# A gated mix of a long convolution and an MLP: the same operations in another order on every engine, with other PSUM banks

## The chip, the cores and the metric

The kernel runs on one core of a Trainium2 chip. The metric is the device time of one execution in microseconds (us). The kernel's five queues are those of TensorE (PE, matmuls and transposes), ScalarE (ACT, activations and copies), VectorE (DVE, elementwise work), GpSimd (POOL) and SyncE (SP, which only issues transfers). ACT and POOL issue transfers too. Each queue is worked off in its order, and an instruction whose semaphore isn't there yet holds up all that stand behind it in its queue.

## The reference

From a sequence of S = 2048 rows of D = 640 channels the kernel computes two results `a` and `b`, and mixes them with a gate `g` of each row. `a` is a short causal filter along the sequence (4 taps), times `v`, then a long convolution along the sequence by FFT, times `q`. `b` is a mixer: layer norm, a matrix, GELU, a shift by one or two rows of each quarter of the channels, a matrix, and then an MLP of width 1536.

```python
def _A_ref(q, k, v, shift_k, ssm_k, ssm_D):
    ...
    for t in range(ks):
        k_shift = k_shift + k_pad[:, t:t + S, :] * shift_k[:, ks - 1 - t][None, None, :]
    kv = k_shift * v
    ...
    y_f = kv_f * kf_f[None, :, :, :]
    y = (lambda x, s, axes=(-2,-1): jnp.fft.irfft2(x, s=s, axes=axes).astype(jnp.bfloat16))(y_f, (1, L), axes=(1, 2))[:, 0, :S, :]
    y = y + kv * ssm_D[None, None, :]
    return q * y

def _B_ref(x, w1, w2, w3, w4):
    h = _gelu(_layernorm(x, axis=-1) @ w1)
    ...
    hs = jnp.concatenate([g0, g1, g2, g3], axis=-1) @ w2
    x1 = x + hs
    h2 = _gelu(_layernorm(x1, axis=-1) @ w3) @ w4
    return x1 + h2

x = A_q
g = _sigmoid((x * gate_w).sum(-1, keepdims=True))
a = _A_ref(x, A_k, A_v, A_shift_k, A_ssm_k, A_ssm_D)
b = _B_ref(x, B_w1, B_w2, B_w3, B_w4)
return g * a + (1 - g) * b
```

## The kernel before

The kernel is recorded first and ordered afterwards. Calls such as `ln1`, `mm1`, `h_fold` or `final` record operations, numbered from 0 to 1199 in the order of the calls; each has its engine, its function and its predecessors (who wrote what it reads, who still reads what it overwrites). An operation of PE can hold several matmuls. The helpers `mm` (L635), `act` (L625), `tt` (L615), `ts` (L620) and `dma` (L238) record nearly all of it, so that the profile shows these few lines; an operation is told from another by its shape, and below by its number.

The stages, by the names of the calls:

- `x_load`, `ln1`, `mm1`, `mmg`, `gate`: rows of `q` are loaded, normalised (statistics on DVE, the power on POOL), turned by PE transposes whose copies ACT makes (`pe_turn`, L846), multiplied by w1 (4 chunks of 512 rows) and put through GELU by ACT. PE first runs 28 warm-up matmuls (L658), and a tiny sum of the gate's weights (`gsum`).
- `h_load`, `h_fold`, `h_chunk` (5 blocks of 128 channels): the transform of the long filter as matmuls with folded cosine and sine tables; `kv_load`, `kv_fold`, `x_fwd` the same for the filtered `k` times `v`: taps on ACT, sums and folds on DVE, a transposing transfer on SP, matmuls on PE, copies on ACT. `combine` folds blocks in the frequency domain on DVE.
- `mm2`, `ln2` (16 tiles of 128 rows): the second matrix, the residual on DVE, the second layer norm on ACT, DVE and POOL, and a transposing transfer on SP.
- `mm3` (4 chunks of 512 rows, 12 tiles of 5 matmuls of 512 columns, GELU on ACT) and `mm4` (16 tiles of 128 rows, two halves of 12 or 13 matmuls of 320 columns). A chunk's mm4 needs its mm3, and the next chunk's mm3 overwrites what mm4 reads. ACT scales the result by 1 − g, and POOL adds it to the output with an accumulating transfer; `base` puts the residual there before.
- `unit(hh, c)`: the products of the spectra on DVE for one half hh of the channels, the sums by accumulating transfers of POOL.
- `final(hh, c, q, k)`: 16 blocks, 8 for each half hh. In one block PE makes two inverse halves of four matmuls each (a PSUM tile of two banks, class `inv`), ACT copies them to SBUF, DVE forms the sum and the difference, PE reverses the rows of the difference with one matmul (the flip, a PSUM tile of one bank, class `fl`), ACT copies that with the gate's scale, and DVE multiplies by `q`. For k < 12 POOL adds the block to the output, for k ≥ 12 DVE adds the residual and SP stores the block.

Of the last blocks these numbers matter below. final(0, 1, 0): 1078 copy of the inverse, 1079 sum, 1080 difference, 1081 flip, 1082 the flip's copy, 1083 the multiplication. 1092 and 1093 are flip and copy of final(0, 1, 1), with 1094 its multiplication; 1116 is the multiplication of final(0, 0, 1). From 1118 on all belong to hh = 1: 1136 and 1137 are the inverse halves of final(1, 2, 0) and 1138 their copy; 1127 and 1128 those of final(1, 3, 1). 1020, 1021, 1026 and 1027 are DVE's last operations of the spectral products for hh = 1. 960 and 961 are the halves of the last mm4 tile, 962 its copy.

What the order comes from: `SEQUENCE` (L452 to L515) lists all 1200 numbers by hand; each engine's queue is this list, cut to that engine. `PLACES` (L517 to L522) gives each of the 213 PSUM tiles, in the order of recording, its first bank of eight. `schedule` (L255) walks the list and makes the first matmul of a tile wait for all users on other engines of the tile that had its banks before:

```python
for b in range(t.place, t.place + t.n):
    if tenant[b] is not None:
        for u in tenant[b].users:
            if ops[u].eng != "pe":
                o.preds.setdefault(u, False)
    tenant[b] = t
```

`emit` (L276) writes the queues with a semaphore wait for each predecessor on another engine that isn't known to be done already. So both lists set waits: the one by what stands ahead in the same queue, the other by the banks.

Of the kernel before, what the change touches and what calls it, by code (L numbers as in the profile page):

```python
# [414 lines left out]
def bass_gated_mix__ssm_conv_h3__mixer_s_mlp__prompt_kernel(  # L415
# [32 lines left out]
    def ps(n, cls):  # L448
# [3 lines left out]
    SEQUENCE = [40, 58, 3, 1, 38, 8, 41, 59, 7, 6, 5, 9, 42, 4, 2, 0, 39, 60, 10, 11, 61, 12, 46, 13, 43, 141, 14, 15, 142, 16,  # L452
# [672 lines left out]

    sched = P.schedule(SEQUENCE, PLACES)
    with nc.Block() as block:  # L1127
# [29 lines left out]
```

## Time and profile before

| | us |
|---|---|
| three runs | 231.78, 232.71, 232.36 |
| median | 232.36 |
| the profiled execution | 232.63 |
| its span in the trace | 230.84 |
| busy in it: PE, DVE, ACT, POOL | 216.46, 210.77, 185.74, 73.06 |
| waiting times of ACT for PE (L635), of PE's weight loads for ACT | 24.7, 13.6 |

The profile's page gives busy times and, in its fourth part, the chain of work that ended last, followed back from the last instruction. A timeline has one row for each run of like instructions: start, length, engine, line, operation, output and input, count, and in brackets the idle time before it with what ended that. A table of windows has for each stretch of time the busy time of the engines with the number of instructions in brackets, then the granted clock of PE (1.00 is full), the share of the transfer engines and GB/s. Groups of instructions have the count, then the busy time with the mean in ns of one, then the idle time just before them. PEld is the weight load that overlaps the matmuls. Matmuls are pipelined, so that one's recorded length is more than the step from its start to the next one's.

### The profile page before, as it was taken

What the parts mean: (1) busy time and instruction counts of PE and PEld (TensorE: products, weight loads), DVE (VectorE), ACT (ScalarE), POOL (GpSimd) and SP (SyncE); (2) the same over time, 40 slices, a digit from 0 to 9 for tenths busy, and PEclk for the clock granted to TensorE, in tenths of its full rate; (3) what the DMA queues carried; (4) which work ended last, traced back from release to release, by engine and by line L of the source; (5) the groups of instructions that cost most, each with busy time, mean ns of one, the idle gap of its engine ahead of it and who ended that gap; (6) DMA issues with size and microseconds to landing.
All of it is one profiled execution on the core that took longest, in us unless ns stands there. A gap on an engine that the chain in (4) does not pass through costs nothing.

```text
span 230.8 us, 3937 instructions
## 1 busy us (share of the span) xinstructions
PE 216.5 (94%) x1455; PEld 127.2 (55%) x1455; DVE 210.8 (91%) x372; ACT 185.7 (80%) x352; POOL 73.1 (32%) x76
## 2 busy tenths in 40 slices
PE   6998899999999999999999999999999999999960
PEld 2576564674464454444765457654666645677630
DVE  5997699999899988979889999999998999999892
ACT  2289869999999999999979878967998368354990
POOL 1223000070230210320295205173118135255962
PEclk9999999999999999999999999999999999999995
DMA  5999948987596999985399776899949949999997
GB/s 180 389 240 265 228 173 151 284 199 165 99 218 180 156 198 275 304 186 122 75 203 189 201 142 126 134 181 208 298 101 183 214 97 164 187 165 118 110 145 141
DMA packets 73937, 42.67 MB, mean 185 GB/s; under 512 B 53945, under 2 KB 69182, under 8 KB 73918
## 3 DMA queue, kind: packets, MB, share of 16 engines
q1 hardware_dynamic: 64912, 30.55, 53.7%
q0 software_dynamic: 8832, 11.80, 34.0%
q8 instruction: 11, 0.18, 0.3%
q10 hardware_dynamic: 174, 0.07, 0.2%
q14 instruction: 8, 0.07, 0.1%
HBM read 14.88 MB, written 6.55 MB: 93 GB/s over the span
## 4 chain that ended last, share of the span: by engine, by line
PE 69%; ACT 26%; DVE 2%; issue 1%; DVEq 0%; ACTq 0%
PE PSall L635 65%; ACT arena L625 26%; PE PSall L658 3%; DVE arena L615 1%; PE PSall L846 1%; DVE arena L655 0%; DVEq L1127 0%; PE PSall L690 0%; DVE arena L646 0%; DVE arena L648 0%; ACTq L364 0%; DVE arena L662 0%
## 5 line engine op out<-in xcount | busy, mean ns | idle before, releaser
L635 PE MATMUL PSall<-arena 128*128 128x320 bf16 (+4 forms) x1341 | 204.2, 310 | 4.6 <-ACT arena L625 2.2
L635 PEld LDWEIGHTS PSall<-arena 128*128 128x128 bf16 x1341 | 119.8, 98 | 87.4 <-ACT arena L625 13.6
L615 DVE TENSOR_TENSOR arena<-arena 128x2560 bf16<-128x2560 bf16 (+7 forms) x201 | 162.8, 861 | 4.9 <-ACT arena L625 2.0
L625 ACT ACTIVATE arena<-PSall 128x512 bf16<-128x512 f32 (+9 forms) x187 | 107.5, 636 | 19.4 <-PE PSall L635 11.1
L625 ACT ACTIVATE arena<-arena 128x1 f32<-128x1 f32 (+5 forms) x115 | 69.5, 646 | 4.0 <-DVE arena L615 2.2
L816 POOL TENSOR_TENSOR arena<-arena 128x1 f32<-128x1 f32 (+1 forms) x26 | 24.1, 954 | 71.5 <-DVE arena L620 71.4
L238 POOL DMA_DIRECT2D out_dram<-arena x28 | 31.3, 1241 | 37.9 <-ACT arena L625 32.9
L625 ACT ACTIVATE arena<-PSall,arena 128x640 bf16<-128x640 f32 (+1 forms) x32 | 20.3, 658 | 13.7 <-PE PSall L635 13.6
L620 DVE TENSOR_SCALAR arena<-arena 128x640 bf16<-128x640 bf16 (+6 forms) x75 | 24.8, 361 | 3.9 <-ACT arena L625 2.8
L238 POOL DMA_DIRECT2D arena<-arena x12 | 16.6, 1384 | 29.9 <-DVE arena L615 29.9
L914 DVE SCALAR_TENSOR_TENSOR arena<-PSall,arena 128x640 bf16<-128x640 f32 x16 | 13.0, 819 | 3.8 <-PE PSall L635 3.8
L812 DVE BATCH_NORM_STATS2 arena<-arena 128x6 f32<-128x320 bf16 x32 | 14.4, 481 | 1.5 <-DMA arena<-in_A_q_dram 1.5
L658 PE MATMUL PSall<-arena 128*128 128x512 bf16 x28 | 9.7, 478 | 1.8 <-DVE arena L655 1.8
L846 PE MATMUL PSall<-arena 128*128 128x128 bf16 x80 | 7.1, 220 | 1.5 <-ACT arena L625 1.3
L846 PEld LDWEIGHTS PSall<-arena 128*128 128x128 bf16 x80 | 5.1, 97 | 3.7 <-ACT arena L625 2.7
L620 POOL TENSOR_SCALAR arena<-arena 128x16 f32<-128x16 f32 x3 | 2.6, 856 | 11.3 <-ACT arena L625 11.3
L658 PEld LDWEIGHTS PSall<-arena 128*128 128x128 bf16 x28 | 2.9, 116 | 5.0 <-issue 2.5
L615 POOL TENSOR_TENSOR arena<-arena 128x16 f32<-128x16 f32 x3 | 4.2, 1391 | 2.4 <-DVE arena L620 2.2
L625 ACT ACTIVATION_READ_ACCUMULATOR arena<-arena 128x1 f32 x16 | 3.5, 218 | 0.0
L664 ACT ACT_TABLE_LOAD x1 | 1.3, 1283 | 2.1 <-issue 2.1
L813 DVE BATCH_NORM_AGGREGATE arena<-arena 128x2 f32<-128x12 f32 x16 | 2.6, 192 | 0.2
L914 DVE DVE_READ_ACCUMULATOR arena<-PSall,arena 128x1 f32 x16 | 1.3, 82 | 0.0
(19 smaller groups left out, 3.4 us busy)
## 6 DMA issues: line engine op xcount, KB each, us to landing
arena<-arena POOLq DMA_DIRECT2D x12, 640.0 KB, 6.3
arena<-in_A_q_dram SPq DMA_DIRECT2D x14, 320.0 KB, 6.2
out_dram<-arena POOLq DMA_DIRECT2D x20, 160.0 KB, 4.4
arena<-in_A_ssm_k_dram SPq DMA_DIRECT2D x5, 512.0 KB, 5.2
arena<-in_B_w_dram SPq DMA_DIRECT2D x1, 1920.0 KB, 8.2
out_dram<-arena SPq DMA_DIRECT2D x10, 160.0 KB, 3.0
arena<-in_B_w_dram SPq DMA_DIRECT2D x1, 1152.0 KB, 6.2
out_dram<-arena SPq DMA_DIRECT2D x12, 80.0 KB, 2.8
```

The lines of the kernel that those rows point to most:

```text
L238: fn = lambda e: e.dma_start(out, in_, **kw)
L615: P.op(eng, lambda e: e.tensor_tensor(o, real(a), real(b), op), [a, b], [o], dve_ns(o, [a, b], 2) if eng == "dve" else 500)
L620: P.op(eng, lambda e: e.tensor_scalar(o, real(a), s1, s2, op0=op0, **({} if op1 is None else {"op1": op1})), [a] + aps, [o], dve_ns(o, [a] ...
L625: P.op("act", lambda e: e.activation(real(o), real(a), f, bias=bias, scale=scale, **({"accum_out": accum} if accum is not None else {})), ...
L635: fns.append(lambda e, l=l, r=r, i=i: e.matmul(real(o), l, r, start=(i == 0), stop=(i == last)))
L658: P.op("pe", lambda e: e.matmul(real(pw), warm[:, 0:128], warm[:, 128:640], start=True, stop=True), [warm], [pw], 427.0)
L664: P.op("act", lambda e: e.activation(tjunk[:, 1:2], ones[:, 0:1], ACTF.Gelu_apprx_tanh), [ones[:, 0:1]], [tjunk[:, 1:2]], 1700)
L812: P.op("dve", lambda e, o=o, i=i: e.bn_stats(o, i), [i], [o], 400)
L813: P.op("dve", lambda e: e.bn_aggr(bna[:, t, :], bns[k]), [bns[k]], [bna[:, t, :]], 120)
L816: P.op("pool", lambda g: g.tensor_tensor(o, a, e, ALU.pow), [a, e], [o], dur)
L846: P.op("pe", [lambda e, c=c, pb=pb, xn=xn: e.transpose(real(pb)[:, 128 * c:128 * (c + 1)], xn[:, 128 * c:128 * (c + 1)], ident) for c in r ...
L914: P.op("dve", lambda e: e.scalar_tensor_tensor(x, real(pr), 1.0, x, op0=ALU.mult, op1=ALU.add, accum_out=st[1, 0][:, t:t + 1]), [pr, x], [ ...
```

## The change

Both lists are replaced by others; no other line differs. `SEQUENCE` is another permutation of the same 1200 numbers that keeps every operation behind those it depends on. The median operation moves by 10 places and the farthest by 400. On PE 289 of 340 places of the queue hold another operation than before, on ACT 310 of 339, on DVE 308 of 356, on POOL 43 of 72, on SP 61 of 93. `PLACES` gives 174 of the 213 tiles another bank. Instructions, shapes, data and buffers in SBUF are the same.

The beginnings and the ends of the lists, the lines with ln2-11's and ln2-12's transfers (719 and 730) and the statistics of ln2-12 (726) among them, and the banks:

```diff
-    SEQUENCE = [40, 58, 3, 1, 38, 8, 41, 59, 7, 6, 5, 9, 42, 4, 2, 0, 39, 60, 10, 11, 61, 12, 46, 13, 43, 141, 14, 15, 142, 16,
-                17, 62, 18, 202, 19, 63, 327, 64, 68, 65, 305, 53, 69, 20, 66, 54, 21, 55, 203, 22, 67, 23, 70,
-                24, 49, 72, 56, 71, 78, 73, 51, 79, 25, 74, 26, 50, 27, 80, 28, 84, 75, 29, 52, 85, 94, 81, 96,
-                525, 82, 98, 100, 83, 143, 30, 76, 147, 31, 77, 146, 144, 102, 157, 104, 103, 145, 148, 105, 86,
-                106, 88, 57, 101, 87, 108, 47, 89, 160, 109, 32, 107, 33, 99, 91, 97, 110, 90, 149, 158, 150, 92,
-                161, 95, 34, 93, 35, 205, 136, 36, 306, 208, 113, 131, 111, 154, 114, 151, 119, 112, 155, 204,
...
-                813, 864, 723, 715, 716, 654, 726, 824, 865, 727, 717, 718, 804, 736, 655, 656, 805, 806, 708,
-                883, 657, 815, 928, 719, 877, 807, 670, 728, 757, 729, 929, 823, 730, 870, 878, 822, 866, 1030,
...
-                979, 1078, 1011, 1106, 1039, 1021, 960, 980, 1024, 981, 961, 1020, 1051, 1091, 1022, 1026, 1013,
-                1136, 962, 1079, 1114, 1127, 1080, 1115, 1128, 963, 1028, 1116, 1023, 1092, 1027, 1081, 1145,
-                1093, 1117, 1129, 1137, 1094, 1082, 1146, 1130, 1095, 1029, 1131, 1187, 1083, 1138, 1174, 1147,
-                1139, 1084, 1132, 1188, 1140, 1133, 1148, 1164, 1149, 1040, 1189, 1134, 1150, 1165, 1151, 1190,
-                1135, 1175, 1191, 1166, 1194, 1152, 1118, 1176, 1167, 1141, 1192, 1153, 1168, 1119, 1142, 1177,
-                1154, 1181, 1120, 1178, 1195, 1155, 1182, 1193, 1196, 1143, 1179, 1169, 1156, 1197, 1183, 1121,
-                1144, 1180, 1122, 1157, 1170, 1123, 1158, 1124, 1184, 1159, 1198, 1125, 1160, 1199, 1185, 1161,
-                1186, 1126, 1171, 1162, 1172, 1163, 1173]
-    PLACES = [0, 1, 1, 2, 6, 5, 3, 2, 3, 4, 5, 6, 7, 6, 7, 1, 4, 1, 0, 7, 5, 1, 6, 6, 3, 2, 0, 5, 5, 2, 4, 5, 0, 7, 6, 0, 6, 6,
-                2, 6, 6, 5, 7, 6, 3, 6, 3, 7, 2, 3, 7, 1, 0, 1, 0, 7, 1, 1, 1, 0, 4, 4, 6, 6, 0, 2, 2, 2, 6, 4, 4,
-                6, 4, 6, 4, 6, 2, 4, 2, 0, 2, 0, 0, 4, 0, 4, 4, 2, 0, 3, 5, 3, 2, 6, 2, 4, 4, 7, 3, 4, 6, 2, 2, 2,
-                4, 6, 4, 2, 0, 6, 0, 0, 6, 2, 6, 0, 0, 2, 2, 6, 0, 4, 0, 2, 6, 0, 0, 6, 6, 0, 0, 6, 6, 4, 2, 3, 4,
-                1, 4, 2, 5, 5, 5, 4, 0, 0, 2, 4, 6, 4, 5, 2, 5, 4, 3, 4, 5, 3, 2, 2, 4, 4, 2, 6, 6, 6, 2, 1, 3, 0,
-                7, 1, 7, 0, 1, 7, 6, 0, 2, 4, 2, 4, 7, 6, 2, 6, 0, 6, 4, 0, 6, 4, 7, 4, 6, 2, 7, 2, 3, 4, 2, 2, 0,
-                0, 2, 4, 2, 0, 2, 4, 0, 6, 1]
+    SEQUENCE = [40, 58, 8, 41, 3, 5, 0, 9, 59, 38, 2, 37, 1, 39, 10, 60, 11, 61, 12, 13, 42, 46, 43, 14, 141, 15, 16, 142, 17, 18,
+                62, 19, 203, 20, 63, 202, 64, 68, 65, 305, 53, 69, 21, 66, 55, 22, 54, 327, 23, 4, 24, 67, 7, 70,
+                51, 72, 71, 78, 73, 525, 79, 25, 74, 26, 27, 80, 28, 84, 75, 94, 85, 81, 96, 29, 82, 98, 100, 83,
+                147, 99, 76, 30, 146, 77, 31, 32, 86, 88, 56, 87, 101, 47, 57, 97, 143, 95, 110, 144, 89, 111,
+                145, 102, 161, 113, 33, 148, 34, 90, 91, 104, 149, 208, 92, 112, 150, 35, 207, 93, 36, 106, 209,
+                158, 108, 114, 131, 103, 151, 154, 152, 133, 308, 123, 153, 115, 48, 205, 127, 105, 160, 135, 155,
...
+                663, 686, 814, 864, 813, 723, 806, 726, 816, 734, 727, 865, 746, 712, 824, 882, 728, 729, 715,
+                866, 805, 730, 716, 871, 807, 815, 717, 718, 883, 958, 817, 719, 928, 822, 1041, 876, 884, 1030,
...
+                1009, 1037, 1077, 1038, 972, 968, 1091, 1008, 969, 973, 1024, 978, 1010, 974, 1011, 1078, 975,
+                1104, 1025, 979, 1105, 960, 1079, 980, 1027, 1106, 1026, 1029, 981, 1013, 961, 1039, 1012, 1051,
+                1021, 1080, 1023, 1020, 1092, 1081, 962, 1136, 1137, 1093, 963, 1028, 1127, 1094, 1138, 1128,
+                1095, 1082, 1187, 1129, 1083, 1188, 1139, 1022, 1140, 1145, 1084, 1189, 1130, 1141, 1131, 1146,
+                1142, 1190, 1174, 1194, 1147, 1195, 1040, 1132, 1191, 1175, 1196, 1143, 1133, 1164, 1148, 1176,
+                1134, 1144, 1165, 1149, 1177, 1118, 1135, 1178, 1166, 1181, 1150, 1119, 1182, 1151, 1167, 1183,
+                1154, 1168, 1120, 1152, 1169, 1155, 1170, 1121, 1153, 1179, 1122, 1192, 1156, 1171, 1123, 1124,
+                1172, 1180, 1173, 1125, 1193, 1157, 1184, 1126, 1158, 1185, 1159, 1197, 1186, 1160, 1198, 1199,
+                1161, 1162, 1163]
+    PLACES = [0, 1, 3, 1, 5, 1, 5, 1, 2, 3, 4, 2, 4, 1, 0, 3, 6, 5, 3, 3, 3, 4, 7, 7, 5, 4, 2, 2, 2, 3, 2, 0, 0, 2, 1, 6, 5, 0,
+                5, 4, 4, 5, 4, 5, 1, 5, 7, 5, 6, 2, 7, 7, 4, 6, 6, 1, 0, 1, 6, 6, 0, 0, 2, 4, 6, 0, 2, 4, 2, 4, 2,
+                6, 4, 0, 4, 0, 4, 6, 2, 4, 2, 6, 6, 2, 0, 0, 4, 2, 2, 3, 6, 2, 1, 5, 0, 1, 3, 3, 1, 2, 4, 2, 4, 2,
+                0, 6, 6, 0, 4, 6, 4, 4, 0, 2, 6, 6, 0, 0, 4, 2, 6, 6, 2, 6, 6, 6, 6, 0, 2, 0, 2, 6, 0, 5, 4, 1, 5,
+                4, 6, 0, 4, 4, 0, 5, 1, 4, 0, 4, 6, 7, 1, 1, 6, 7, 6, 6, 7, 6, 1, 0, 0, 4, 2, 2, 2, 4, 6, 3, 6, 7,
+                6, 0, 1, 0, 2, 5, 3, 6, 4, 2, 4, 4, 7, 2, 4, 0, 2, 6, 1, 0, 5, 6, 4, 4, 6, 6, 7, 0, 5, 6, 5, 0, 5,
+                6, 5, 6, 0, 6, 5, 0, 4, 0, 0]
```

At the end, the inverse tiles of hh = 1 lie in four pairs of banks before (0, 2, 4, 6 as the first of two) and in two after (0 and 6), and the flips' tiles mostly in banks 0 to 3 before and in bank 5 after.

95 rows, old and new, of the table SEQUENCE are left out of this document.

## The prediction

> **What bounds the kernel now.** I read the page first: the busy shares and the chain that ended last.
>
> ```profile
> span 230.8 us, 3937 instructions
> PE 216.5 (94%) x1455; PEld 127.2 (55%) x1455; DVE 210.8 (91%) x372; ACT 185.7 (80%) x352; POOL 73.1 (32%) x76
> PE 69%; ACT 26%; DVE 2%; issue 1%; DVEq 0%; ACTq 0%
> ```
>
> TensorE (PE) and VectorE (DVE) are both busy for over nine tenths of the span, so an order alone can win little: the span less PE's busy time is 14.3 us, less DVE's 20.0 us, and part of both is the start and the last transfer. The chain in order of time says where which engine decides.
>
> ```profile
> 1.77 4.87 PE PSall L658 x11
> ...
> 11.23 0.71 ACT arena L625
> ...
> 81.66 8.57 PE PSall L635 x50
> ...
> 90.44 130.62 PE PSall L635 x796
> ...
> 223.67 2.64 DVE arena L615 x8
> 226.31 0.40 DVEq L1127
> ```
>
> Up to 11 us PE's warm-up and first transposes decide, from there to 81.66 mostly the copies on ScalarE (ACT), from there to 221.06 almost nothing but PE's matmuls, and at the end DVE. Busy time by stage agrees (columns: PE, PEld, DVE, ACT, POOL, then the clock):
>
> ```profile
> 0.00:20.00 20.00, 17.35 (x169) 10.90 (x169) 17.12 (x65) 10.25 (x29) 4.18 (x10) 1.00 0.94 282
> 20.00:40.00 20.00, 17.65 (x137) 11.11 (x138) 16.78 (x38) 16.64 (x32) 1.50 (x2) 1.00 0.84 183
> 40.00:80.00 40.00, 39.31 (x290) 22.38 (x289) 37.76 (x84) 39.81 (x75) 10.23 (x10) 1.00 0.81 186
> 80.00:100.00 20.00, 19.13 (x100) 9.17 (x98) 17.21 (x34) 20.00 (x34) 4.25 (x6) 1.00 1.05 255
> 100.00:150.00 50.00, 50.00 (x302) 29.05 (x301) 48.21 (x48) 44.47 (x85) 15.38 (x16) 1.00 0.77 150
> 150.00:200.00 50.00, 50.00 (x301) 28.72 (x299) 48.37 (x54) 37.73 (x70) 20.50 (x20) 1.00 0.92 181
> ```
>
> From 100 to 200 us PE shows no gap at all. A reordering can win there only what it won before 100 us, and whatever makes PE wait there is lost. ACT's idle time before 40 us (9.75 in the first 20 us, 3.36 in the next) is what a better start could fetch; between 40 and 100 ACT is full.
>
> **The change part by part.** It removes and adds no operation; the working is where each list puts them. I walked the new queues by hand, stretch by stretch, with each operation's duration from its row before.
>
> *Start, to 40 us.* The new list puts the gate sum's matmuls and one warm matmul later, and lets ACT evacuate one tile of mm1 (operation 99) between the first two transposes' copies. These ACT rows show what it waits for now:
>
> ```profile
> 11.23 0.70 ACT L625 ACTIVATE arena<-PSall 128x640 bf16<-128x640 bf16 x1 [1.99 <-PE PSall L846]
> 12.48 0.79 ACT L625 ACTIVATE arena<-PSall 128x128 bf16<-128x128 f32 x4 [0.55 <-PE PSall L635]
> ...
> 28.65 2.34 ACT L625 ACTIVATE arena<-PSall 128x640 bf16<-128x640 bf16 x5 [0.62 <-PE PSall L846]
> 31.45 0.70 ACT L625 ACTIVATE arena<-PSall 128x640 bf16<-128x640 bf16 x1 [0.46 <-PE PSall L846]
> 33.89 1.19 ACT L625 ACTIVATE arena<-PSall 32x512 bf16<-32x512 f32 x2 [1.73 <-PE PSall L635]
> ```
>
> The filled-in evacuation takes 0.79/4 = 0.20 of the 1.99, and PE's fewer matmuls bring the turn some 0.3 forward: about 0.5. At 27 to 34 the three waits (2.81 together) become one of about 1.9 in the new order, for mm1's first matmul of the third chunk behind two of mm2. ACT is thus up to 0.5 + 0.9 = 1.4 ahead at most and by my walk some 0.9, PE 0.3, DVE 0.5. From below the bound is 0: what PE does not pass on.
>
> *40 to 100 us.* ACT is full there, so its lead should stay. Against it stand new waits in DVE's queue, which runs in order: kv_fold-3 now stands behind two more copies of h_chunk on ACT, and a mean copy is 0.64.
>
> ```profile
> L625 ACT ACTIVATE arena<-PSall 128x512 bf16<-128x512 f32 (+9 forms) x187 | 107.5, 636 | 19.4 <-PE PSall L635 11.1
> ...
> 99.24 0.57 DVE L620 TENSOR_SCALAR arena<-arena 128x1 f32<-128x1 f32 x2 [1.30 <-ACT arena L625]
> ...
> 110.38 2.55 DVE L615 TENSOR_TENSOR arena<-arena 128x2048 bf16<-128x2048 bf16 x3 [0.84 <-DMA arena<-in_A_v_dram]
> ...
> 116.67 1.49 DVE L615 TENSOR_TENSOR arena<-arena 128x2560 bf16<-128x2560 bf16 x1 [0.57 <-DMA arena<-arena]
> ```
>
> Two copies are 1.3 against the 1.30 that DVE now waits at 99.24 and that becomes about 0.7: a loss of 0.6 or so. *100 to 150 us:* v's last load is issued earlier on SP, which frees DVE of the 0.84 and, with the work shifted, of the 0.57. But ln2-12's statistics on DVE now stand ahead of ln2-11's and wait for an ACT operation that x_fwd-4's last matmuls hold back; that gives most of the 1.41 back. Over both stretches I take 0 for PE, which sets the end and has no gap there to close; bounds: 0.9 won (ACT's lead reaches PE through its waits before 90 us) and 1.7 lost (below, under the rivals).
>
> *The end.* Here the new list differs most. Now PE runs without a gap through the last matmuls of mm4 into the inverse matmuls of the second half (hh = 1), and squeezes the left-over flips in between:
>
> ```profile
> 211.80 5.45 PE L635 MATMUL PSall<-arena 128*128 128x320 bf16 x38
> ...
> 212.63 1.18 ACT L625 ACTIVATE arena<-PSall,arena 128x640 bf16<-128x640 f32 x2
> ...
> 212.75 0.68 DVE L615 TENSOR_TENSOR arena<-arena 128x320 bf16<-128x320 bf16 x2
> ...
> 213.84 2.80 DVE L615 TENSOR_TENSOR arena<-arena 128x640 bf16<-128x640 bf16 x6 [0.41 <-ACT arena L625]
> 216.91 0.69 DVE L615 TENSOR_TENSOR arena<-arena 128x320 bf16<-128x320 bf16 x2 [0.27 <-ACT arena L625]
> ```
>
> The second DVE row (212.75, two instructions) holds operations 1079 and 1080, the add and subtract of final(0, 1, 0): 1080 ends at 213.43. Its flip, 1081, is issued after the first inverses of hh = 1. In the new order, flips 1092 and 1081 stand ahead of every inverse of hh = 1, directly behind the last mm4 (which ends before 212.63, where ACT copies it). The durations:
>
> ```profile
> 212.00:220.00 8.00, 8.00 (x60) 1.00 0.99 109
> ...
> L625 ACT ACTIVATE arena<-PSall 128x640 bf16<-128x640 f32 x16 | 10.9, 695 | 1.3 <-PE PSall L635 1.2
> L625 ACT ACTIVATE arena<-PSall,arena 128x320 bf16<-128x320 f32 x16 | 8.2, 528 | 3.4 <-PE PSall L635 3.2
> ...
> L615 DVE TENSOR_TENSOR arena<-arena 128x320 bf16<-128x320 bf16 x40 | 11.8, 321 | 1.0 <-ACT arena L625 0.3 <-DMA out_dram<-arena 0.2
> L615 DVE TENSOR_TENSOR arena<-arena 128x640 bf16<-128x640 bf16 x16 | 7.5, 483 | 0.4 <-ACT arena L625 0.4
> ...
> 215.40:226.80 11.40, 10.41 (x34) 0.93 1.12 142
> ```
>
> A matmul of 320 columns follows the next after 8.00/60 = 0.133 us. DVE reaches 1080 later than now, because 1116 (0.48) has been put ahead of it and one spectral product is merely exchanged for another: 1080 ends at about 213.43 + 0.48 = 213.9. PE waits for it from some 212.6 to 213.95, behind it all sixteen inverses. Then: flip 1081 and the eight matmuls of 1136 and 1137 are issued by 213.95 + 9 × 0.133 = 215.15, the last result is there some 0.2 later, ACT's copy 1138 (0.695) comes ahead of the flip's copy 1082 (0.528): 216.05, then 216.55. DVE's next operation in its queue, 1083, needs 1082. Between 213.9 and 216.55 DVE has only 1020 (0.82) and 1094 (0.48), so it stands still for about 1.4 where it now loses 0.41 + 0.27 = 0.68. From 1083 on DVE is the bound again: the remaining work, the same operations as in the window from 215.40 on, is 10.41 busy, and by the walk about 0.8 of waits for copies and flips, since there are two pairs of inverse banks in place of four and one flip bank most of the time: 216.55 + 10.4 + 0.8 = 227.8. DVE now ends in the pieces from 223.67 to 226.31 and the queue's 0.40: at 226.71. The end costs 227.8 − 226.7 = 1.1. Bounds: 0.2 if no such wait is left (216.55 + 10.4 = 226.95), 3.3 if at the very end one round trip more stands open (copy 0.70, add and subtract 0.64, flip 0.13, copy 0.53: 2.0, and 0.2 for passing it on).
>
> **The sum.** The profiled execution took 232.63 us, 230.84 in its span and 1.79 around it; the median of the runs shown is 232.36, 0.27 below. Start: 0, since ACT's 0.9 must pass the new waits to reach PE, and PE's own 0.3 meets the later 1080 on DVE, which does not come from PE. Middle: 0. End: +1.1. That is 232.63 + 1.1 = 233.7 us.
>
> **The rivals.**
>
> *The lead arrives (faster).* ACT's 0.9 shortens PE's waits before 90 us, and DVE's 0.84 + 0.57 stay won, so that DVE reaches 1080 1.4 earlier, at 212.5, when PE arrives. Then the wait of PE is nearly gone, and the new end costs 0.2 in place of 1.1: 232.63 − 0.9 − 1.4 + 0.2 = 230.5. For it: ACT is full from 40 to 100, so time won ahead of it is not lost in gaps. Against it: PE is the chain from 81.66 on, and DVE's gain of 1.4 can shorten only the end. It decides once DVE is over 0.7 earlier at 1080.
>
> *All cancels (no change).* ACT's lead reaches PE whole (−0.9) and the end costs its 1.1, or neither happens: 232.8.
>
> *PE waits ahead of mm3's third chunk (slower still).* The new list issues ln2-12's transpose on SP ahead of ln2-11's, whose result mm3-2's first matmul needs.
>
> ```profile
> 143.62 2.55 SPq L235 DMA_TRANSPOSE arena<-arena  x2
> ...
> 147.54 1.70 SPq L235 DMA_TRANSPOSE arena<-arena  x1
> ```
>
> The first row ends with ln2-11's, at 146.2; the last is ln2-12's, which came only when its data did. Put ahead it holds the queue for 1.70, and PE, which has no gap from 100 to 212, would lose up to that: 233.7 + 1.7 = 235.4. Against it: one more mm4 half (12 matmuls, 1.6) now lies ahead of mm3-2, which by my walk just covers it.
>
> *Half clock at the end.* The page rows show PE at full clock until 224 and at 0.69 behind its gaps:
>
> ```profile
> 222.00:223.00 1.00, 0.41 (x3) 0.07 (x1) 1.00 (x4) 1.00 (x3) 0.02 (x1) 1.00 1.24 144
> ...
> 224.00:227.00 3.00, 0.31 (x1) 0.10 (x1) 2.71 (x8) 0.86 (x2) 1.49 (x2) 0.69 1.02 172
> ```
>
> In the chain's first row a warm matmul of 512 columns takes 4.87/11 = 0.44, twice the later pace, for 4.87 us. Were the new wait of 1.3 at 212.6 followed by such a stretch, PE would lose 2.4 in it: 233.7 + 2.4 = 236.1. Against it: the clock still stood at 1.00 beside the idle 0.59 of 222 to 223. The Trainium skill, TensorE: Matmul & The Clock Gate, section "Part 1: The HAM clock gate", says that the clock halves after an idle window of about 3.4 us, by which a wait of 1.3 would do nothing; its section "A second HAM failure mode: psum-queue depth-cycling" says that frequent short gaps while cycling through PSUM banks can do it too, which would be this rival. No row of this case shows so short a gap halving the clock.
>
> **How the numbers follow.** A measurement tells 0.5% from no change here, 1.16 us: under 231.2 is faster, over 233.5 slower. The forecast (end decides, 232.9 to 234.6) 0.35, of which 0.10 lies below 233.5; the lead arrives 0.25; all cancels 0.20; PE waits before mm3-2 0.15; half clock 0.05. Faster 0.25; same 0.20 + 0.10 = 0.30; slower 0.25 + 0.15 + 0.05 = 0.45. The likeliest is the forecast, 233.7. The range reaches from the faster rival's 230.5 to just over the stalled case's 235.4, as the end's upper bound (3.3) gives 235.9: 230.5 to 235.9.
>
> **What would show it.** Right: in the new profile PE has one gap of 1 us or more directly behind the last mm4, released by DVE, then DVE a gap of about 1.4 some 2 us later, and DVE's last operation ends 0.9 to 1.5 later than 226.7. The start: ACT's wait ahead of the second turn falls from 1.99 to about 1.5. Wrong: PE without a gap around 212, or PE past mm4's last matmul more than 0.9 before 212.4 (the lead arrived), or a gap of PE between 145 and 155 (the third rival), or a clock below 1.00 before 220.

## The result, and the profile after

Fourteen runs of the new kernel have a median of 234.98 us (234.14 to 236.38), fourteen of the old one 233.0 (231.78 to 234.24). The ratio is 1.0088, with a 95% interval of 1.0064 to 1.0113: the new order is 0.9% slower. Ratios, here and below, leave out executions that ran in a slower state of the chip, as four of the eleven of e3_tail did and the profiled one of e6_pool, which took 458 us. The profiled execution of the new kernel has a span of 232.9 us, 2.1 above the old one's.

The new page's first and fourth part:

```profile
span 232.9 us, 3918 instructions
PE 214.8 (92%) x1443; PEld 127.0 (55%) x1455; DVE 211.4 (91%) x372; ACT 187.1 (80%) x352; POOL 76.5 (33%) x76
...
ACT 39%; PE 33%; DVE 11%; DMA 6%; POOL 5%; issue 2%; SPq 1%; DVEq 0%; POOLq 0%
```

PE is no longer the chain from 81 us to the end: POOL has come in with 5% and transfers (DMA) with 6%, and DVE is up from 2% to 11%. (Twelve of PE's matmul records are missing; the weight loads are complete.) Where the time went is seen in the stages that correspond to those of before (columns: PE, PEld, DVE, ACT, POOL, clock):

```profile
80.00:100.00 20.00, 19.60 (x101) 9.41 (x101) 17.28 (x34) 20.00 (x30) 5.74 (x7) 1.00 1.06 257
100.00:150.00 50.00, 49.71 (x302) 29.19 (x304) 48.61 (x47) 44.91 (x89) 17.71 (x15) 1.00 0.75 154
150.00:200.00 50.00, 47.26 (x273) 26.44 (x275) 46.93 (x54) 35.27 (x65) 21.84 (x19) 1.00 0.94 173
```

Between 150 and 200 us PE is busy for 47.26 of 50, where it had no gap before. The weight loads, 275 against 299, say the same. PE's timeline from 80 us on has these gaps (in brackets):

```profile
90.25 68.17 PE L635 MATMUL PSall<-arena 128*128 128x512 bf16 x384 [0.31 <-ACT arena L625]
159.39 2.33 PE L635 MATMUL PSall<-arena 128*128 128x512 bf16 x10 [0.97 <-ACT arena L625]
163.29 61.83 PE L635 MATMUL PSall<-arena 128*128 128x512 bf16 x403 [1.57 <-ACT arena L625]
226.97 0.31 PE L635 MATMUL PSall<-arena 128*128 128x320 bf16 x1 [1.85 <-DVE arena L615]
```

0.97 + 1.57 = 2.54 us are lost inside mm3-2, and PE has no gap from 163.29 to the last blocks. The chain of waits through this stretch leads to a power on POOL:

```profile
145.10 7.17 DVE arena L615 x6
152.26 0.14 DVE arena L620
152.40 0.07 issue
152.48 4.61 POOL arena L816
157.09 0.84 POOL out_dram L238
157.93 1.24 POOL arena L238
159.16 0.94 POOL out_dram L238
160.11 1.61 POOL arena L816
161.72 0.02 issue
161.74 1.50 ACT arena L625 x3
163.25 0.05 issue
163.29 0.39 PE PSall L635
```

The 4.61 us are operation 749: the power by which ln2-14 gets its 1/sqrt, one column of 128 rows. Of the sixteen powers of ln2 in this profile the shortest take 0.55 us, and the longest but this one 2.74. ACT's operation 750 waits for it, and what stands behind 750 in ACT's queue are the GELU copies that free PE's banks. The second gap lies behind a second power, 760 of ln2-15: it stands behind 749 and three transfers in POOL's queue, and ACT's 761 waits for it until 161.74. ACT's rows beside it (two kinds: one column for 750, 128x512 for the copies):

```profile
157.12 1.25 ACT L625 ACTIVATE arena<-arena 128x1 f32<-128x1 f32 x2 [1.62 <-POOL arena L816]
158.27 1.55 ACT L625 ACTIVATE arena<-PSall 128x512 bf16<-128x512 f32 x3
161.74 1.01 ACT L625 ACTIVATE arena<-arena 128x1 f32<-128x1 f32 x2 [1.92 <-POOL arena L816]
```

Before, the power was early and its reader late, as POOL's row of 749 and 760 and ACT's row of 750 in the old profile show:

```profile
155.06 3.01 POOL L816 TENSOR_TENSOR arena<-arena 128x1 f32<-128x1 f32 x2
```

```profile
163.84 0.28 ACT L625 ACTIVATE arena<-arena 128x1 f32<-128x1 f32 x1
```

Some 7 us lay between the end of 749 (156.6) and 750; in the new order 750 starts as soon as 749 ends. What DVE did while 749 took 4.61 us, in the new profile:

```profile
152.19 0.20 DVE L620 TENSOR_SCALAR arena<-arena 128x1 f32<-128x1 f32 x1
152.31 4.35 DVE L615 TENSOR_TENSOR arena<-arena 128x2560 bf16<-128x2560 bf16 x4
156.58 0.32 DVE L620 TENSOR_SCALAR arena<-arena 128x1 f32<-128x1 f32 x2
```

Four elementwise operations on two tensors (832, 833, 671, 835) without a break, until 156.66. 749 ends at 157.09, 0.43 later. The experiments test whether these four are what holds it up.

At the end there is nothing new on PE: directly behind the last mm4 it goes on with the flips. DVE's last row is

```profile
224.07 4.82 DVE L615 TENSOR_TENSOR arena<-arena 128x320 bf16<-128x320 bf16 x13 [0.19 <-DMA out_dram<-arena]
```

and so ends at 228.89. From the copy of the last mm4 tile (212.63 before, 214.88 now) to DVE's end it took 14.1 before and takes 14.0 now.

### The profile page after: what moved, and what is told of

The parts are those of the page before. It is cut to its first block, busy times and chain, and to the rows that moved or that the text cites. A ratio compares the mean times of both kernels' runs of the same rounds, so it can differ in the third digit from the quotient of the medians.

```text
span 232.9 us, 3918 instructions
## 1 busy us (share of the span) xinstructions
PE 214.8 (92%) x1443; PEld 127.0 (55%) x1455; DVE 211.4 (91%) x372; ACT 187.1 (80%) x352; POOL 76.5 (33%) x76
## 4 chain that ended last, share of the span: by engine, by line
ACT 39%; PE 33%; DVE 11%; DMA 6%; POOL 5%; issue 2%; SPq 1%; DVEq 0%; POOLq 0%
ACT arena L625 39%; PE PSall L635 33%; DVE arena L615 11%; DMA out_dram<-arena 3%; POOL arena L816 3%; DMA arena<-in_B_w_dram 3%; POOL out_dram L238 2%; SPq L238 1%; POOL arena L238 1%; PE PSall L846 1%; DVE arena L620 0%; PE PSall L658 0%; DVEq L364 0%; POOLq L364 0%
## 5 line engine op out<-in xcount | busy, mean ns | idle before, releaser
L635 PE MATMUL PSall<-arena 128*128 128x320 bf16 (+4 forms) x1330 | 203.5, 309 | 8.8 <-ACT arena L625 5.2
L615 DVE TENSOR_TENSOR arena<-arena 128x2560 bf16<-128x2560 bf16 (+6 forms) x201 | 163.7, 861 | 6.8 <-DMA arena<-arena 2.6
L635 PEld LDWEIGHTS PSall<-arena 128*128 128x128 bf16 x1341 | 119.8, 98 | 91.3 <-ACT arena L625 18.0
L625 ACT ACTIVATE arena<-PSall 128x512 bf16<-128x512 f32 (+9 forms) x187 | 108.6, 640 | 15.4 <-PE PSall L635 10.2
L625 ACT ACTIVATE arena<-arena 128x640 bf16<-128x640 bf16 (+5 forms) x115 | 70.6, 657 | 8.8 <-DVE arena L615 4.6
L816 POOL TENSOR_TENSOR arena<-arena 128x1 f32<-128x1 f32 (+1 forms) x26 | 32.3, 1298 | 89.0 <-DVE arena L620 89.0
L238 POOL DMA_DIRECT2D arena<-arena x12 | 15.3, 1275 | 34.0 <-DVE arena L615 33.9
L812 DVE BATCH_NORM_STATS2 arena<-arena 128x6 f32<-128x320 bf16 x32 | 14.1, 478 | 1.9 <-DMA arena<-in_A_q_dram 1.9
L658 PE MATMUL PSall<-arena 128*128 128x512 bf16 x27 | 8.3, 437 | 1.6 <-DVE arena L655 1.6
L620 POOL TENSOR_SCALAR arena<-arena 128x16 f32<-128x16 f32 x3 | 1.5, 513 | 4.9 <-ACT arena L625 4.9
L655 DVE MEMSET arena<- 128x640 bf16 x1 | 0.6, 592 | 0.9 <-PEq L1142 0.9
```

Of the source, the lines that this page charges most:

```text
L238: fn = lambda e: e.dma_start(out, in_, **kw)
L615: P.op(eng, lambda e: e.tensor_tensor(o, real(a), real(b), op), [a, b], [o], dve_ns(o, [a, b], 2) if eng == "dve" else 500)
L620: P.op(eng, lambda e: e.tensor_scalar(o, real(a), s1, s2, op0=op0, **({} if op1 is None else {"op1": op1})), [a] + aps, [o], dve_ns(o, [a] ...
L625: P.op("act", lambda e: e.activation(real(o), real(a), f, bias=bias, scale=scale, **({"accum_out": accum} if accum is not None else {})), ...
L635: fns.append(lambda e, l=l, r=r, i=i: e.matmul(real(o), l, r, start=(i == 0), stop=(i == last)))
L658: P.op("pe", lambda e: e.matmul(real(pw), warm[:, 0:128], warm[:, 128:640], start=True, stop=True), [warm], [pw], 427.0)
```

## The experiments

The new and the old list are near enough to each other that a list may begin with the one and go on with the other without two tiles meeting in a bank. So the change could be put in by stretches. Lines of the trace in these kernels, but for e11_new, lie five lower than before (L630 for L635, L610 for L615, L811 for L816). Each ratio is to runs of the old kernel on the same chip, with its 95% interval; the new kernel's own is 1.0088.

**One stretch at a time.** e1_head has the new start alone, e2_mid the new middle, e3_tail the new end, each with its banks:

```diff
-SEQUENCE = OLD
+e1_head: NEW[:850], then the rest in OLD's order
+e2_mid:  OLD[:850], then NEW's order up to its place 1089, then the rest in OLD's order
+e3_tail: OLD[:1090], then the rest in NEW's order
```

> Places 0 to 849 of the list are the new order's (to about 147 us), the rest is the old one's, with the banks that go with each. Theory (the loss lies between 152 and 164 us, where a power on POOL is late): the start changes next to nothing, 0 to 0.9 us faster than before, that is 232.1 to 233.0 beside a before of 233.0. Rival (the loss is built up earlier and only shows there): at least 1 us slower than before.

> Only places 850 to 1089 (about 148 to 210 us) are the new order's, with its banks; start and end are the old one's. Theory: all of the loss is here, 2 to 2.5 us slower than before, with PE gaps of about 1 and 1.6 us near 158 and 162 and a DVE wait of about 2.5 us behind a transfer of POOL. Rival (the end costs 1.1, as predicted, and the middle only what PE's lead makes good): 1 us slower or less.

> Only places from 1090 on (about 209 us) are the new order's. By the prediction's step: PE waits about 1.3 us for operation 1080 behind the last mm4, the end comes 1.1 us later than before (bounds 0.2 and 3.3). Rival (in the new profile PE did not wait there, and the end took 0.3 less behind the last mm4 than before): 0.3 us faster to 0.2 slower.

Measured: start 1.0015 (0.9982 to 1.0048), middle 1.0129 (1.0078 to 1.018), end 1.0041 (0.9993 to 1.0088). The start is worth nothing that can be told, as expected. The middle alone is 3 us slower, more than the whole change, but not by the waits that were expected. In e2_mid POOL's late power is another one, 716 of ln2-11, which the old order has:

```profile
141.88 3.32 POOL L811 TENSOR_TENSOR arena<-arena 128x1 f32<-128x1 f32 x1
```

In the old profile it took 0.56:

```profile
140.98 0.56 POOL L816 TENSOR_TENSOR arena<-arena 128x1 f32<-128x1 f32 x1
```

The operations on ACT that need this power start only at 145.24, after 3.25 us of waiting. Further back in ACT's queue stands the copy 878, which frees the banks of mm3-2's first tile; it ends at 150.74, and PE waits ahead of mm3-2 and once more inside it:

```profile
150.79 5.18 PE L630 MATMUL PSall<-arena 128*128 128x512 bf16 x28 [1.09 <-ACT arena L620]
157.47 7.83 PE L630 MATMUL PSall<-arena 128*128 128x512 bf16 x36 [1.50 <-ACT arena L620]
```

So e2_mid does not say what the new middle costs by itself; it shows the same kind of lateness at another power. It shows one thing more. DVE's queue beside 749 is here the new one, and the same four operations (832, 833, 671, 835) run there without a break. Yet 749 takes 1.74, ends 0.42 behind the first of them, and PE has no gap at the two tiles where the new kernel lost its 2.54:

```profile
156.60 1.74 POOL L811 TENSOR_TENSOR arena<-arena 128x1 f32<-128x1 f32 x1
```

```profile
156.44 4.35 DVE L610 TENSOR_TENSOR arena<-arena 128x2560 bf16<-128x2560 bf16 x4
```

So the four operations alone do not make 749 late. What else has to come together is not known.

The end behaves in e3_tail as the prediction's step had it, PE and DVE both:

```profile
199.77 12.25 PE L630 MATMUL PSall<-arena 128*128 128x320 bf16 x89
213.57 0.31 PE L630 MATMUL PSall<-arena 128*128 128x320 bf16 x1 [1.55 <-DVE arena L610]
```

```profile
214.89 0.49 DVE L610 TENSOR_TENSOR arena<-arena 128x640 bf16<-128x640 bf16 x1 [0.64 <-ACT arena L620]
216.96 1.32 DVE L610 TENSOR_TENSOR arena<-arena 128x640 bf16<-128x640 bf16 x4 [1.57 <-ACT arena L620]
```

PE waits 1.55 for 1080 (1.3 was worked out), DVE 1.57 ahead of 1083 (1.4). The time rises by 0.4%, 1.0 us (1.1), though its interval just takes in no change. The step is seen in the trace behind the old middle; PE's wait does not happen behind the new one.

**A break for POOL.** e4_gap moves two one-column operations of DVE, which have to be done at some time anyway, between the first and the second of the four:

```diff
 DVE's queue of the new kernel
-748, 832, 833, 671, 835, 759, 737, 670
+748, 832, 759, 737, 833, 671, 835, 670
```

> The new kernel with two DVE operations of one column each (759 and 737, the statistics of ln2-15 and ln2-13) moved ahead, right behind 832. Theory (the power 749 on POOL gets its turn only when DVE runs no tensor_tensor): 749 ends near 154.0 instead of 157.1, PE's gaps of 0.97 and 1.57 and DVE's wait of 2.56 shrink to a quarter or less, and the time falls by 1.5 to 2.5 us from the new kernel's 235.0. Rival (the power is slow for reasons on POOL itself): 749 still takes over 4 us, no change of time.

Measured: 0.9962 (0.9926 to 0.9999), that is 1.25% below the new kernel (0.9962/1.0088 = 0.9875), and below the old one. POOL's row of 749, then PE's from 150 to 170 us:

```profile
153.91 1.74 POOL L811 TENSOR_TENSOR arena<-arena 128x1 f32<-128x1 f32 x1 [2.31 <-DVE arena L615]
```

```profile
149.80 20.44 PE L630 MATMUL PSall<-arena 128*128 128x320 bf16 x113
```

749 takes 1.74 and ends 0.4 behind 832, and PE's two gaps and DVE's wait of 2.56 are gone. No work was taken out and what each operation depends on stayed the same, only DVE's order changed. That 759 comes earlier is not the gain by itself: in the new kernel it was done at 156.78, and POOL came to the power that needs it, 760, only 2.2 us later. The gain, 2.9 us, is above the expected 1.5 to 2.5.

**Who waits for the power.** e5_act leaves POOL and DVE alone and moves the power's readers on ACT behind the copies; e6_pool instead moves a transfer of POOL, for which DVE waits 2.56 us in the new kernel, ahead of the power:

```diff
 e5_act, ACT's queue
-750, 751, 907, 903, 887, 761, 1064, 891, 878, 901, 970, 905, 897
+907, 903, 887, 750, 751, 1064, 891, 878, 901, 970, 905, 897, 761
 e6_pool, POOL's queue
-749, 873, 827
+827, 749, 873
```

> The new kernel with three ACT operations moved back in ACT's queue: 750 and 751 (ln2-14's, which wait for the power 749 on POOL) behind 887, and 761 (ln2-15's) behind 897. Nothing else. Theory (PE loses 2.5 us because the copies of mm3-2's tiles stand behind these three on ACT, and DVE loses 2.56 because the accumulating transfer 827 stands behind 749 on POOL; two victims of one late power): PE's gaps at 158 and 162 vanish, 749 still takes over 4 us and DVE's wait stays about 2.5; the time falls by 1 to 2.5 us, since PE sets the end until DVE's lateness shows at operation 1080. Rival (PE's gaps come from the banks alone): gaps and time unchanged.

> The new kernel with POOL's transfer 827 moved ahead of the power 749 in POOL's queue. Nothing else. Theory: DVE's wait of 2.56 at 163.6 vanishes; 749, ready later by the transfer's 1.5 us, still ends with the same DVE operation as before (near 157.1), so that PE's gaps stay within 0.5 us of 0.97 and 1.57, and the time stays within 0.7 us of the new kernel's. Rival (749 takes 4.6 us by itself): it ends 1.5 us later and PE loses 1.5 more.

e5_act: 1.0003 (0.9964 to 1.0041), 0.85% below the new kernel, 2.0 us. 749 still takes 4.61, and PE keeps one gap in place of two:

```profile
153.03 4.61 POOL L811 TENSOR_TENSOR arena<-arena 128x1 f32<-128x1 f32 x1 [2.31 <-DVE arena L615]
```

```profile
162.01 8.17 PE L630 MATMUL PSall<-arena 128*128 128x512 bf16 x49 [0.87 <-ACT arena L620]
```

With 749 as late as before, the first gap is gone and the second is 0.87 in place of 1.57: that they come from what stands behind the power in ACT's queue, and not from the banks alone, is shown for the first gap and for half of the second. What is left lies behind 750, 751 and 1064, which stand ahead of the copy 891 that PE needs and no longer wait. The expectation for DVE missed: its wait for 827's transfer was down to 0.18, though POOL issued it as late as before.

e6_pool: 0.9973 (0.9945 to 1.0001), a gain of 2.7 us where 0.7 was the limit. For a trace that can be read beside the others the kernel was run once more.

> The same kernel as e6_pool, whose profiled execution ran at half pace throughout and can't be read beside the others; its time was 2.7 us below the new kernel's where theory expected 0.7 at most. Explanation to be tested: 749, asked for 1.5 us later, gets its turn at an earlier DVE end than 157.1 (near 155.6), so that PE's gaps go too. Rival: 749 ends near 157.1 and PE's gaps stay, and the gain comes from DVE's wait alone. The time again 0.2 to 0.5% below before.

Measured: 1.0012 (0.9975 to 1.005). The explanation fell; of the first theory, that 749 ends behind the same DVE operation stood:

```profile
154.32 1.19 POOL L238 DMA_DIRECT2D arena<-arena  x1 [2.39 <-DVE arena L615]
155.06 3.78 POOL L811 TENSOR_TENSOR arena<-arena 128x1 f32<-128x1 f32 x1
```

749 began later, took 3.78 and ended at 158.84, again 0.42 behind 835. PE's gaps were 0.96 and 0.16, so that the second did not stay as that theory had it. Between them the two measurements put this edit at 0.75 to 1.15% below the new kernel; the profile accounts for the 1.4 us of PE's second gap, and the rest is not explained.

**Both cures, and the old end.** e8_both has the edits of e4_gap and e6_pool; e9_oldend has e4_gap's and, from place 1090 on, the old order.

> The new kernel with the edits of e4_gap and of e6_pool together. Theory (both cure the same late power): no more than either alone, 0.3 to 0.5% faster than before, no PE gap above 0.5 us between 100 and 210. Rival (they cure two things): 0.8% or more faster than before.

> The new kernel with the edit of e4_gap, and from place 1090 on the old order and its banks. Theory (the new end costs something only where DVE comes to 1080 after PE, as in e3_tail; in e4_gap it comes before): the same time as e4_gap within 0.2%, 0.2 to 0.6% faster than before. Rival (the new end costs its 1.1 us everywhere): 0.4 to 0.5% faster than e4_gap, 0.8 to 0.9% faster than before.

e8_both: 0.9945 (0.9914 to 0.9977). It beats both kernels, the old one by 0.55% (1.3 us), and 749 takes 1.04 us in it. Whether the second edit adds anything to e4_gap's 0.9962 can't be told. The gain is one of the average: the fastest executions of the two kernels are alike (232.27 us, the old one's 232.40 in the same series), while the slowest are 233.80 and 235.71, and the two traces, with spans of 230.9 and 230.8 us, do not show where it comes from. e9_oldend: 0.9987 (0.9944 to 1.0029), no faster than e4_gap: the new end costs nothing here that can be told. PE's rows from 99 us on in e8_both:

```profile
99.64 122.74 PE L630 MATMUL PSall<-arena 128*128 128x512 bf16 x762
223.06 0.31 PE L630 MATMUL PSall<-arena 128*128 128x320 bf16 x1 [0.68 <-DVE arena L610]
```

There is no gap of PE from 99.64 to 222.38, through the last mm4 and past 1081.

**ACT's order at the end.** DVE has two waits there, 0.75 and 0.84, for copies of ACT. e7_best, with e4_gap's edit, puts those copies first:

```diff
 ACT's queue
-962, 1093, 1028, 1138, 1082, 1129
+1093, 1082, 1138, 1028, 1129, 962
 PLACES, the inverse tile of 1127
-6
+2
```

> The new kernel with the edit of e4_gap, and at the end ACT's copies in the order 1093, 1082, 1138, 1028, 1129, 962 with 1127's tile in banks 2 and 3, so that the copies that DVE waits for come first. Theory: DVE's waits of 0.75 and 0.84 behind 1020 and 1094 shrink to about 0.6 together, 0.5 to 1 us faster than e4_gap, some 0.7% faster than before. Rival (the end is bound by PE and ACT alike, the wait only moves to the next copy): same time as e4_gap, within 0.3 us.

Measured: 1.0056 (1.0029 to 1.0082), 0.9% slower than e4_gap. The copy of the last mm4 tile, 962, is now late; POOL's queue stands behind its transfer, and DVE waits for buffers that those transfers free:

```profile
218.43 3.37 POOL L238 DMA_DIRECT2D out_dram<-arena  x3 [3.77 <-ACT arena L620]
```

```profile
223.81 1.09 DVE L610 TENSOR_TENSOR arena<-arena 128x320 bf16<-128x320 bf16 x3 [0.94 <-DMA out_dram<-arena]
226.90 1.61 DVE L610 TENSOR_TENSOR arena<-arena 128x320 bf16<-128x320 bf16 x4 [2.01 <-DMA out_dram<-arena]
```

The waits ahead of 1094 and 1083 went to 0.20 and nothing, but 1139 and 1190 waited 0.49 and 0.59 for copies in their place, as the rival had it. The waits for transfers, which neither theory had, came on top: these 2.95, and 0.73 ahead of 1130.

**The power's length by place, and the new kernel once more.** e10_gap2 puts the two one-column operations one product later than e4_gap; e11_new is the new kernel unchanged.

```diff
 DVE's queue of the new kernel
-748, 832, 833, 671, 835, 759, 737, 670
+748, 832, 833, 759, 737, 671, 835, 670
```

> As e4_gap, with the two DVE operations of one column behind 833 instead of 832, one product later. Theory (749 gets its turn at the end of the DVE product that these follow): 749 takes about 3.1 us, between the 1.7 of e4_gap and the 4.6 of the new kernel, ending 0.4 us behind 833; PE's two gaps shrink to 1 us or less together and the time lies between that of e4_gap and that of the new kernel. Rival (749 is served at any end of a product by chance): its length has no relation to the place of the two.

> The new kernel itself, once more. Theory (749's lateness belongs to the order and not to that one execution): 749 again takes 4.6 us and ends 0.4 us behind 835, PE's gaps near 158 and 162 are there again with some 2.5 us together, and the time is 0.6 to 1.1% above before. Rival: 749 varies from execution to execution.

The first row is POOL's in e10_gap2, the second in e11_new:

```profile
153.36 3.14 POOL L811 TENSOR_TENSOR arena<-arena 128x1 f32<-128x1 f32 x1 [2.31 <-DVE arena L615]
```

```profile
153.18 4.61 POOL L816 TENSOR_TENSOR arena<-arena 128x1 f32<-128x1 f32 x1 [2.31 <-DVE arena L620]
```

3.14 against an expected 3.1, ending 0.43 behind 833: the power ends behind the product that the two one-column operations follow, as in e4_gap, e7_best and e9_oldend. In e11_new the 4.61 came again, PE's gaps with it (0.96 and 1.57); its ratio is 1.0037 (0.9979 to 1.0095), which takes in 1.0088 and no change as well. So the lateness of 749 belongs to the new order as a whole and not to one execution; that the order of DVE at this place does not settle it alone, e2_mid shows.

The time of e10_gap2 missed by far: 1.0149 (1.009 to 1.0209), slower than the new kernel (237.13 to 238.54 us, where e11_new beside it took 234.75 to 235.81). The power was shorter, yet 827's transfer landed later, and PE got a new gap:

```profile
168.63 1.56 DVE L610 TENSOR_TENSOR arena<-arena 128x1280 bf16<-128x1280 bf16 x2 [4.11 <-DMA arena<-arena]
```

```profile
162.78 10.47 PE L630 MATMUL PSall<-arena 128*128 128x512 bf16 x67 [1.30 <-ACT arena L620]
175.30 4.97 PE L630 MATMUL PSall<-arena 128*128 128x320 bf16 x23 [2.05 <-ACT arena L620]
```

DVE waits 4.11 for a transfer that POOL issued by 158.6, earlier than in the new kernel (159.2, a wait of 2.56). It landed next to a transposing transfer and two others that SP issued between 157.8 and 161.8; in e5_act these began only at 160.8, and DVE waited 0.18. That the transfers slow each other is an argument from these times; it was not tried alone.

## Why the prediction was right, and where it was not

The forecast was slower, 233.7 us; it is slower, 234.98. What it said of the room held: an order can win little here, and what PE waits between 100 and 200 us is lost. But it put the loss at the end, and it arose in the middle. That the time came near is luck: a loss of 1.1 us that did not come was made up for by one of 2.5 that was not listed. By its own signs the mechanism was wrong, since PE has no gap around 212.

- *The start, 0 taken.* ACT's rows of the new profile show the filled-in tile, and the second turn's copy at 10.47 instead of 11.23:

```profile
9.91 0.28 ACT L625 ACTIVATE arena<-PSall 128x128 bf16<-128x128 f32 x1 [2.00 <-PE PSall L635]
10.47 1.28 ACT L625 ACTIVATE arena<-PSall 128x640 bf16<-128x640 bf16 x5 [0.28 <-PE PSall L846]
```

  Nothing of these 0.76 us reaches the time: e1_head is within 0.5% of before on either side.
- *40 to 150 us, 0 taken.* PE's busy time from 80 to 150 is 69.31 against 69.13 before. Right.
- *The middle, 0 for PE with 1.7 as the worst.* This is the step that failed: PE lost 2.54 us, by a wait that the prediction did not list. It had asked of each moved operation what stands behind it in its queue, for DVE, SP and PE, and not of 750 on ACT, where the 7 us of slack behind a power went to nothing; and it took each operation's duration from its row before, by which 749 has 1.56 us, where it took 4.61. The rival with the wait ahead of mm3's third chunk had the right chunk and the wrong place: in the new kernel that matmul came without a gap. In e1_head and e2_mid 0.89 and 1.09 us were lost ahead of it, but for ACT's copy 878 and not for the transpose.
- *The end, +1.1.* PE's wait for 1080 is right in place and size, by e3_tail, but only behind the old middle: there 1080 ends 1.97 us behind the last weight load of mm4. In the new kernel, in e4_gap and in e8_both it ends 0.13 behind that load, whether PE comes late or not; in the new kernel DVE, with its wait of 2.56, came as late as PE. At this load DVE has 13.5 us of work left in the new order and had 15.4 in the old one, since the new middle does more of it earlier. The prediction took DVE's place at 212 us from the old order. The rest of the step came: DVE stood still for 0.75 and 0.84 ahead of 1094 and 1083 (1.4 was worked out), and from 1083 to its end it took 11.43 us (11.25). Counted from the last mm4 tile's copy, the whole term measured −0.1.
- *The lead arrives*, the faster rival, has its half for DVE in e8_both: 1080 ends at 212.34, 1.1 us earlier than before, as PE arrives. PE's own lead is not seen there (the last weight load of mm4 ends at 212.21, before at 212.03), and the gain of 1.3 us is less than the 2.1 that the rival had. *Half clock* did not occur: the clock stood at 1.00 up to 220 us, and in e3_tail, with its wait of 1.55, too.

What stays open: why the old order's power 716 takes 0.56 in one kernel and 3.32 in another, why 749 takes 4.61 in the new kernel and 1.74 in e2_mid beside the same four operations, what picks the DVE operation behind which a waiting power is served, and how 827's transfer came to take from under 5 to 10 us.

## What to carry to other kernels

A small operation on a slow helper engine needs slack behind it when its reader stands ahead of the bank copies in an in-order queue: 7 us of slack were here worth 2.5 us of TensorE's time. Before reordering VectorE, look for unbroken runs of two-input operations beside a GpSimd operation that someone waits for; moving two one-column operations into such a run took the kernel from 0.9% slower to 0.4% faster. Such a run need not do harm (it did none in e2_mid), so look at the power's row in the trace first. A step worked out for one stretch holds only with the arrival times that the rest of the new order gives it.

## What the runs showed of the hardware

A power on GpSimd over 128 rows takes some 0.55 us when VectorE leaves it room, and up to 4.61 beside VectorE's elementwise operations on two tensors in SBUF. In thirteen profiles of this study (all but e6_pool's) 117 of the 208 powers of ln2 took over 1.3 us, and 116 of them ended 0.39 to 0.46 us behind the end of some VectorE operation. A waiting power is not always served at the first such end: 749 was passed over at three in a row, behind 832, 833 and 671, in the new kernel (twice), in e5_act and in e6_again. In e2_mid, with the same four operations in a row, it took 1.74 and ended 0.42 behind the first. The Trainium skill, SBUF — State Buffer, section "Who interferes with whom", says that a VectorE instruction with two inputs in SBUF contends with a GpSimd instruction that reads SBUF, and that the port they share is an exclusive lock. The trace agrees with the blocking, with 0.43 us from the end of VectorE's 835 to the power's end; that the blocked one can lose the next three turns as well is beyond what that section says.
